# Softmax weights written to DRAM in pairs of steps and read back in 1 KB pieces

## The chip, the cores and the metric

The kernel runs on one core of one Trainium2 chip. The metric is the device time of one execution in microseconds (us). The core has five engines that run side by side: TensorE (PE in the profile, with its weight loads listed as PEld), VectorE (DVE), ScalarE (ACT), GpSimd (POOL) and SyncE (SP), which here issues nearly all DMAs. All arrays are float32.

## The reference

The kernel computes x + s * g for x of shape 2048 x 512. s is attention over a cached window, g the silu of a gated MLP with a mixing matrix over the positions. Cut to what matters here:

```
xn = layernorm(x)                                  # (2048, 512)
# s: 32 heads of size 128, keys and values: the last 512 of the cache
q = xn @ wq                                        # per head (2048, 128)
p = softmax(q @ k.T * 128 ** -0.5)                 # per head (2048, 512)
s = concat(p @ v) @ wo                             # (2048, 512)
# g
z = gelu(xn @ w_in);  z1, z2 = halves of z         # 688 columns each
g = silu((z1 * (w_sp @ layernorm(z2) + b_sp)) @ w_out)
return x + s * g
```

The change concerns p alone, on its way from the softmax to p @ v.

## The kernel before

**Numbers.** Each matmul of float32 accuracy is three: every operand is split into a high part (float32r, made by a cast on ScalarE) and a rest (what is left, made by a subtraction, `rest`, L59). `mm3` (L63 to L67) issues high x high, high x rest and rest x high into one PSUM buffer.

**Stages.** After layernorm and the first products of z the attention runs from about 55 to 1500 us of the span. The mixing and the output follow (after 1500 us); they aren't touched by the change.

**Blocks and steps.** The attention works on 128 blocks, each one head and 512 queries, and each block has four steps of 128 queries. There are 512 steps; one loop (L672 to L722) runs over them, and writes the order of the instructions by hand: nothing is reordered by a scheduler. A step's work is spread over several turns of that loop. For step t with t = 4b + j:

- `score(t)` (turn t, L466 to L475): three matmuls give 128 queries x 512 keys in PSUM. VectorE takes the row maximum (nm), ScalarE the exponential into the tile prob and the row sums. The division by the sums is left to the end.
- `turn(t)` (turn t + 1, L477 to L488): VectorE's transpose works on squares of 32 x 32, so it turns p within each square only, into the tile pB. SyncE writes pB to DRAM (p_dram, 4 x 128 x 512 for a block), 256 KB at a time, rows of 2 KB.
- `turned(b)` (turn 4b + 6, L490 to L494): four DMAs, one for each quarter of the keys, bring the block back so that the squares come to stand in their places: into 32 partitions each of the tile pL (keys on partitions, 2048 values each). A contiguous piece is 128 values, 512 bytes. In the loop `turned` stands ahead of `turn` of the same turn: the reads of block b are issued ahead of the write of step 1 of block b + 1.
- `shares(b, c)` (turn 4b + c + 10, L496 to L502): for each 128 keys ScalarE casts the high part (pT_h) out of pL, in runs of 32 values, and GpSimd makes the rest (pT_l).
- `pv(b, c)` (turn 4b + c + 12, L504): three matmuls for each quarter of the keys accumulate o, 128 columns of the head x 512 queries, in PSUM (ps_a). `pv_out` (L509) casts it to oT_h on ScalarE and appends the rest oT_l to a list `late`, which VectorE takes at the end of the turn, after its transpose.
- `outp(b, j)` (turn 4b + j + 17, L518): three matmuls with the head's wo; VectorE multiplies by the reciprocal sums and adds to sacc (L528).

Beside this, PE computes the next q (`q_products`, L437 to L447, a scheme of seven products over blocks of two heads), and GpSimd and ScalarE split the weights that are loaded for coming heads. The loads of weights (`load_piece`, L102, and `load_q`, L407), 256 KB each, stand at the head of a turn; the pieces of heads come at turns that are 0, 5 and 6 modulo 8, two pieces for q at 7 modulo 16. From turn 30 to 214 the second half of x is prepared and stored in DRAM (x_dram), and at turns 231 to 245 it is fetched.

**Queues.** All these DMAs go through SyncE's one queue, in the order of the program. SyncE waits for the buffers and data of a DMA before it issues it, and what comes after it in the program waits too.

**Buffers.** prob has 3 buffers, pB 4 of 2 KB per partition, p_dram 3 blocks, pL 2, pT_h and pT_l 4 each. The pool `ap` of these tiles has 2 buffers where a tile names no other number.

Of the kernel before, what the change touches and what calls it, by code (L numbers as in the profile page):

```python
# [8 lines left out]
F32 = mybir.dt.float32  # L9
# [8 lines left out]
P = 128  # L18
# [18 lines left out]
Q = 32  # L37
# [3 lines left out]
def mixer_kernel(ctx: ExitStack, tc: tile.TileContext, x, wh, w_in, w_sp, b_sp, w_out, out):  # L41
# [8 lines left out]
    nc = tc.nc  # L50
# [3 lines left out]
    dram = ctx.enter_context(tc.tile_pool(name="dram", bufs=1, space=DRAM))  # L54
# [3 lines left out]
    def rest(engine, lo, whole, hi):  # L58
        engine.tensor_tensor(lo, whole, hi.bitcast(F32), op=OP.subtract)  # L59

    late = []
# [25 lines left out]
    ap = att.enter_context(tc.tile_pool(name="ap", bufs=2))  # L87
# [259 lines left out]
    def z1_product(i, n, between=lambda: None):  # L347
        ps = ps_acc.tile([P, 512], F32, name="ps_a") if n else ps_step.tile([P, 512], F32, name="ps_3")
        zmm(ps[:, :NB], i, n, range(2))
        between()  # L350
        zmm(ps[:, :NB], i, n, range(2, NC))
        return ps
# [7 lines left out]
        z1_out(i, n, z1_product(i, n, between))  # L360


    qps, qT, pps, pD, pL, pT, oT, prob, sums = {}, {}, {}, {}, {}, {}, {}, {}, {}

    def where(b):
# [111 lines left out]
    def turn(t):  # L477

        b, j = divmod(t, 4)
        pB = ap.tile([P, 512], F32, name="pB", bufs=4)
        nc.vector.transpose(pB.rearrange("p (k q) -> p k q", q=Q), prob.pop(t))  # L483
        if j == 0:
            pD[b] = dram.tile([4, P, 512], F32, name="p_dram", bufs=3)
        nc.sync.dma_start(pD[b][j], pB)
        if j == 3:
            nc.vector.reciprocal(sums[b], sums[b])  # L488

    def turned(b):  # L490
        pL[b] = ap.tile([P, 16, P], F32, name="pL")
        of = pD.pop(b).rearrange("j (i r) (a f) -> a r (j i) f", i=4, a=4)
        for a in range(4):
            nc.sync.dma_start(pL[b][Q * a:Q * a + Q], of[a])  # L494

    def shares(b, c):  # L496
        hi = ap.tile([P, 512], F32R, name="pT_h", bufs=4)
        lo = ap.tile([P, 512], F32R, name="pT_l", bufs=4)
        p, h, l = pL[b][:, :, Q * c:Q * c + Q], *(t.rearrange("p (i q) -> p i q", q=Q) for t in (hi, lo))
        nc.scalar.copy(h, p)  # L500
        rest(nc.vector if 4 * b + c >= NSTEP - 10 and c % 2 else nc.gpsimd, l, p, h)
        pT[b, c] = (hi, lo)  # L502
# [6 lines left out]
    def pv_out(b, c):  # L509
        if c == 3:  # L510
            hi = ap.tile([P, 512], F32R, name="oT_h")
            lo = ap.tile([P, 512], F32R, name="oT_l")
            ps = pps.pop(b)
            nc.scalar.copy(hi, ps)
            late.append((rest, nc.vector, lo, ps, hi))
            oT[b] = (hi, lo)

    def outp(b, j):  # L518
# [74 lines left out]
    for p in range(4):  # L593
        seq, store = later_x(p)
        for f, ks in seq:
            t = 30 + 13 * n // 5
# [41 lines left out]
    ps = ps_step.tile([P, 512], F32, name="ps_3")  # L638
# [9 lines left out]
    ps = ps_step.tile([P, 512], F32, name="ps_3")  # L648
# [4 lines left out]
    ps = ps_acc.tile([P, 512], F32, name="ps_a")  # L653
# [18 lines left out]
    for t in range(T0, T1):  # L672
# [9 lines left out]
        i = t + XL  # L682
        if i < T8:
            ln_flip(i)
        if 0 <= bm < NBLK:
            shares(bm, cm)
# [10 lines left out]
        g, s = divmod(t + LEAD, 16)  # L697
# [6 lines left out]
        if t in DRAIN:  # L704
            ps = z1_product(*DRAIN[t])
# [4 lines left out]
        if 0 <= bp < NBLK:  # L710
            pv_out(bp, cp)
        if t in DRAIN:
            z1_out(*DRAIN[t], ps)
        if t % 4 == 2 and 0 <= t // 4 - 1 < NBLK:
            turned(t // 4 - 1)
        if 0 <= t - 1 < NSTEP:
            turn(t - 1)
# [7 lines left out]
    ps = z1_product(*LAST[-1])  # L725
# [276 lines left out]
```

## Time and profile before

| | us |
|---|---|
| median of 2 runs | 1877.19 (1876.64 to 1877.74) |
| the profiled execution | 1883.31 |
| its span, first to last instruction | 1881.4 |
| PE busy in the span | 1826.0 |
| VectorE busy | 1397.8 |
| GpSimd busy | 1243.4 |
| ScalarE busy | 1177.5 |

The profile is one execution; busy times are sums over an engine's instructions. Matmuls overlap, and their ends are modelled. The rows of the trace that the prediction quotes are of these kinds. A row of a stretch has its start and end, its length, the busy time and number of instructions of each engine (PE, PEld, VectorE, ScalarE, GpSimd, as far as they have any), the TensorE clock granted, the share of the 16 DMA engines and GB/s. A row of waits has who waited for whom, us in total, times, and the longest. A timeline row has start, length, engine, line, operation, out<-in and, after an x, how many in a row were merged. A GB/s row cuts a stretch into 40 equal slices. A row of a group of instructions has the shapes, the number, the busy time and mean ns of one, and the idle time of the engine ahead of it with what ended it. A row of DMA issues has the number, the size and the median us from issue to landing.

### The profile page before, as it was taken

The page shows a single profiled execution, that of the slowest core. Times are in us where ns is not written, and L with a number is a line of the kernel's source. Part 1 is how long each engine was busy: PE and PEld are TensorE (multiplying, and loading weights), DVE is VectorE, ACT ScalarE, POOL GpSimd, SP SyncE. Part 2 cuts the span into 40 slices and gives each one's busy share as a digit, 9 for nine tenths or more (in the row PEclk, how much of TensorE's full clock was granted, in tenths as well). Part 3 has the DMA queues.
Part 4 walks back from the last instruction along what each step waited for, and adds up shares of the span by engine and source line. Part 5 has one row for each costly group of instructions (what it writes and reads, how often), then busy time and mean ns, then how long its engine had stood idle before and what let it go on. Part 6 is the DMA issues. An engine that isn't in the chain of part 4 may idle for free.

```text
span 1881.4 us, 28888 instructions
## 1 busy us (share of the span) xinstructions
PE 1826.0 (97%) x8658; PEld 1549.1 (82%) x8658; DVE 1397.8 (74%) x2369; ACT 1177.5 (63%) x2631; POOL 1243.4 (66%) x1185
## 2 busy tenths in 40 slices
PE   8999999999999998899999999999999999999999
PEld 7777878878778776677888888888887899999998
DVE  5687988989889886788888888888887555333333
ACT  4666767767767765667777777777776444333322
POOL 3787888889888886778888888888886343000000
PEclk9999999999999999999999999999999999999999
DMA  5799999999999999999999999999999825554532
GB/s 178 194 288 239 241 273 246 267 260 265 256 257 241 255 253 293 247 271 247 262 240 253 254 248 248 242 256 249 260 236 260 238 92 164 164 168 139 179 114 89
DMA packets 445565, 429.22 MB, mean 228 GB/s; under 512 B 26368, under 2 KB 318976, under 8 KB 444256
## 3 DMA queue, kind: packets, MB, share of 16 engines
q1 hardware_dynamic: 440800, 421.74, 84.3%
q10 hardware_dynamic: 4608, 5.64, 0.9%
q8 instruction: 68, 1.11, 0.2%
q14 instruction: 89, 0.73, 0.1%
HBM read 260.55 MB, written 166.72 MB: 227 GB/s over the span
## 4 chain that ended last, share of the span: by engine, by line
PE 71%; DMA 13%; ACT 5%; DVE 5%; POOL 3%; issue 3%; SPq 1%; ACTq 0%; POOLq 0%; DVEq 0%
PE ps_a L446 10%; PE ps L65 9%; PE ps L67 9%; PE ps L66 9%; PE ps_a L66 6%; DMA p_dram<-pB 6%; PE ps_a L67 6%; PE ps_a L65 6%; DMA pL<-p_dram 5%; PE ps_g L66 4%; PE ps_g L67 4%; PE ps_g L65 4%; ACT prob L475 2%; POOL pT_l L59 1%; DVE nm L473 1%
## 5 line engine op out<-in xcount | busy, mean ns | idle before, releaser
L59 POOL TENSOR_TENSOR pT_l<-pL,pT_h 128x512 fp32r<-128x512 f32 x507 | 658.3, 1299 | 248.4 <-ACT pT_h L500 160.7
L475 ACT ACTIVATE prob<-ps,nm 128x512 f32<-128x512 f32 x512 | 352.1, 688 | 218.7 <-DVE nm L473 215.3
L500 ACT CAST pT_h<-pL 128x512 fp32r<-128x512 f32 x512 | 317.5, 620 | 193.8 <-DMA pL<-p_dram 128.3
L528 DVE SCALAR_TENSOR_TENSOR sacc<-ps,sums,sacc 128x512 f32<-128x512 f32 x496 | 368.3, 743 | 93.1 <-PE ps L67 91.3
L483 DVE STREAM_TRANSPOSE pB<-prob 128x512 f32<-128x512 f32 x512 | 359.3, 702 | 77.5 <-DMA p_dram<-pB 65.5
L446 PE MATMUL ps_a<-x,x 128*128 128x512 f32 x1302 | 377.7, 390 | 0.6 <-DVE oT_l L59 0.4
L473 DVE TENSOR_REDUCE nm<-ps 128x1 f32<-128x512 f32 x512 | 340.2, 664 | 8.5 <-PE ps L67 8.5
L446 PEld LDWEIGHTS ps_a<-x,x 128*128 128x128 f32 x1302 | 245.2, 188 | 53.7 <-DVE oT_l L59 2.3
L59 POOL TENSOR_TENSOR wl<-raw,wh 128x512 fp32r<-128x512 f32 x192 | 249.9, 1302 | 9.0 <-ACT wh L141 9.0
L66 PE MATMUL ps_a<-pT_l,wh 128*128 128x512 f32 x512 | 205.7, 402 | 19.0 <-POOL pT_l L59 18.4
L65 PE MATMUL ps_a<-pT_h,wh 128*128 128x512 f32 x512 | 201.6, 394 | 19.3 <-ACT pT_h L500 19.3
L65 PE MATMUL ps<-wh,qT_h 128*128 128x512 f32 x512 | 202.1, 395 | 3.8 <-DVE sacc L528 2.5
L65 PE MATMUL ps<-wh,oT_h 128*128 128x512 f32 x512 | 200.4, 391 | 0.3 <-DVE sacc L528 0.3
L67 PE MATMUL ps<-wh,oT_l 128*128 128x512 f32 x512 | 200.4, 391 | 0.0
L67 PE MATMUL ps_a<-pT_h,wl 128*128 128x512 f32 x512 | 200.4, 391 | 0.0
L66 PE MATMUL ps<-wl,qT_h 128*128 128x512 f32 x512 | 200.2, 391 | 0.0
L67 PE MATMUL ps<-wh,qT_l 128*128 128x512 f32 x512 | 200.2, 391 | 0.0
L66 PE MATMUL ps<-wl,oT_h 128*128 128x512 f32 x512 | 200.2, 391 | 0.0
L66 PE MATMUL ps_g<-z_l,x 128*128 128x344 f32 x512 | 164.5, 321 | 1.1 <-POOL z_l L59 1.1
L67 PE MATMUL ps_g<-z_h,x 128*128 128x344 f32 x512 | 164.5, 321 | 0.0
L65 PE MATMUL ps_g<-z_h,x 128*128 128x344 f32 x512 | 164.3, 321 | 0.0
L66 PEld LDWEIGHTS ps_a<-pT_l,wh 128*128 128x128 f32 x512 | 96.4, 188 | 56.7 <-POOL pT_l L59 38.2
(203 smaller groups left out, 3229.1 us busy)
## 6 DMA issues: line engine op xcount, KB each, us to landing
p_dram<-pB SPq DMA_DIRECT2D x512, 256.0 KB, 6.0
pL<-p_dram SPq DMA_DIRECT2D x512, 256.0 KB, 5.4
raw<-wh SPq DMA_DIRECT2D x194, 256.0 KB, 6.2
wq<-wh SPq DMA_DIRECT2D x62, 256.0 KB, 6.5
x<-w_sp SPq DMA_DIRECT2D x60, 256.0 KB, 5.8
x_dram<-rawx SPq DMA_DIRECT2D x32, 256.0 KB, 6.4
x<-x_dram SPq DMA_DIRECT2D x28, 256.0 KB, 6.6
u_dram<-uB SPq DMA_DIRECT2D x15, 384.0 KB, 2.3
```

The costliest lines, as they stand in the source:

```text
L59: engine.tensor_tensor(lo, whole, hi.bitcast(F32), op=OP.subtract)
L65: nc.tensor.matmul(ps, lh, rh, start=first, stop=False)
L66: nc.tensor.matmul(ps, lh, rl, start=False, stop=False)
L67: nc.tensor.matmul(ps, ll, rh, start=False, stop=last)
L446: nc.tensor.matmul(qps[g, bank], wt["q", g, k][a][:, c * P:(c + 1) * P], X[g * 2 // H][ORDER[k]][:, b, c], start=first, stop=r == 5, skip_ ...
L473: nc.vector.tensor_reduce(nm, ps, axis=AX.X, op=OP.max, negate=True)
L475: nc.scalar.activation(prob[t], ps, AF.Exp, bias=nm, accum_out=sums[b][:, j:j + 1])
L483: nc.vector.transpose(pB.rearrange("p (k q) -> p k q", q=Q), prob.pop(t))
L500: nc.scalar.copy(h, p)
L528: nc.vector.scalar_tensor_tensor(at, ps, rs, at, op0=OP.mult, op1=OP.add)
```

## The change

A pair of steps now shares one buffer. The tile pB holds, for each of the four quarters of the keys, 128 values of the even step and then 128 of the odd one; it has the pool's 2 buffers of 4 KB instead of 4 of 2 KB. It goes to DRAM after the odd step only, 512 KB at once, rows of 4 KB (p_dram is 2 x 128 x 1024). The four reads of a block take pieces of 256 contiguous values, 1 KB. The queries then stand in another order (two steps interleaved in groups of 32), the matmuls of pv carry that order along, and the casts of o write their results back into the right one. The rest of o is made in two halves.

```diff
+    pB = [None]
@@ turn
-        pB = ap.tile([P, 512], F32, name="pB", bufs=4)
-        nc.vector.transpose(pB.rearrange("p (k q) -> p k q", q=Q), prob.pop(t))
+        if j % 2 == 0:
+            pB[0] = ap.tile([P, 4, 2, P], F32, name="pB")
+        nc.vector.transpose(pB[0][:, :, j % 2, :].rearrange("p a (c q) -> p a c q", q=Q),
+                            prob.pop(t).rearrange("p (a c q) -> p a c q", a=4, q=Q))
         if j == 0:
-            pD[b] = dram.tile([4, P, 512], F32, name="p_dram", bufs=3)
-        nc.sync.dma_start(pD[b][j], pB)
+            pD[b] = dram.tile([2, P, 1024], F32, name="p_dram", bufs=3)
+        if j % 2:
+            nc.sync.dma_start(pD[b][j // 2], pB[0].rearrange("p a j f -> p (a j f)"))
@@ turned
-        pL[b] = ap.tile([P, 16, P], F32, name="pL")
-        of = pD.pop(b).rearrange("j (i r) (a f) -> a r (j i) f", i=4, a=4)
+        pL[b] = ap.tile([P, 8, 256], F32, name="pL")
+        of = pD.pop(b).rearrange("s (i r) (a f) -> a r (s i) f", i=4, a=4)
@@ shares
-        p, h, l = pL[b][:, :, Q * c:Q * c + Q], *(t.rearrange("p (i q) -> p i q", q=Q) for t in (hi, lo))
+        p = pL[b].rearrange("p i (j f) -> p (i j) f", j=2)[:, :, Q * c:Q * c + Q]
+        h, l = (t.rearrange("p (i q) -> p i q", q=Q) for t in (hi, lo))
@@ pv_out
-            ps = pps.pop(b)
-            nc.scalar.copy(hi, ps)
-            late.append((rest, nc.vector, lo, ps, hi))
+            ps = pps.pop(b).rearrange("p (s i j q) -> p s i j q", s=2, i=4, j=2)
+            h, l = (t.rearrange("p (s j i q) -> p s i j q", s=2, i=4, j=2) for t in (hi, lo))
+            nc.scalar.copy(h, ps)
+            for k in range(2):
+                late.append((rest, nc.vector, l[:, k], ps[:, k], h[:, k]))
```

## The prediction

> **What bounds the kernel now.** The page first: the attention stage (slices 2 to 31, about 55 to 1475 us) has PE at 8 to 9 tenths and DMA at 9. Then busy time by stretch, where x counts instructions.
>
> ```profile
> span 1881.4 us, 28888 instructions
> 100.00:900.00 800.00, 764.48 (x3283) 613.54 (x3282) 666.67 (x1132) 555.34 (x1303) 657.17 (x627) 0.99 1.00 259
> 900.00:1400.00 500.00, 500.00 (x2206) 413.81 (x2205) 440.86 (x735) 368.49 (x853) 436.30 (x404) 1.00 0.97 249
> 1400.00:1500.00 100.00, 94.66 (x456) 79.32 (x455) 69.71 (x112) 58.73 (x132) 57.65 (x49) 1.00 0.94 250
> ```
>
> The first numbers are PE, then weight loads, VectorE, ScalarE, GpSimd. From 900 to 1400 us PE is never idle: 2206 matmuls at 0.227 us each. At that rate the 3283 of 100 to 900 us need 744 us and took 800: 56 us are lost there. The same query for the tile pB counts steps:
>
> ```profile
> 100.00:900.00 800.00, 196.30 (x280) 0.99 1.00 259
> 900.00:1400.00 500.00, 132.88 (x190) 1.00 0.97 249
> ```
>
> So 70 blocks of four steps take 11.4 us each in the first part, and 47.5 blocks take 10.53 us in the second. What PE waits for (100 to 1450 us):
>
> ```profile
> PE ps_a L65 <- ACT pT_h L500: 18.6, 10, 5.9
> PE ps_a L66 <- POOL pT_l L59: 15.5, 35, 0.9
> ```
>
> Both are casts of p that came back late, so the round trip of p through DRAM limits the first part. SyncE's own timeline shows that trip; all its transfers go through one queue.
>
> ```profile
> 1000.41 2.23 SPq L486 DMA_DIRECT2D p_dram<-pB  x2
> 1005.77 1.91 SPq L494 DMA_DIRECT2D pL<-p_dram  x4
> 1007.73 2.36 SPq L486 DMA_DIRECT2D p_dram<-pB  x3
> 1010.13 0.46 SPq L102 DMA_DIRECT2D raw<-wh  x1
> 1012.33 0.32 SPq L486 DMA_DIRECT2D p_dram<-pB  x1
> 1012.74 0.38 SPq L102 DMA_DIRECT2D raw<-wh  x1
> 1015.01 1.91 SPq L494 DMA_DIRECT2D pL<-p_dram  x4
> 1016.97 0.49 SPq L486 DMA_DIRECT2D p_dram<-pB  x1
> 1017.50 1.56 SPq L407 DMA_DIRECT2D wq<-wh  x2
> 1019.16 0.40 SPq L486 DMA_DIRECT2D p_dram<-pB  x1
> 1019.60 0.43 SPq L102 DMA_DIRECT2D raw<-wh  x1
> 1020.78 2.96 SPq L486 DMA_DIRECT2D p_dram<-pB  x2
> 1026.94 1.03 SPq L494 DMA_DIRECT2D pL<-p_dram  x2
> ```
>
> A closed loop: the four reads of a block (1005.77) wait until its step 3 has landed; behind them come steps 1, 2, 3 of the next block (x3 from 1007.73), and that step 3 releases the next reads (1015.01). Step 0 is written while SyncE would else only wait (1012.33): its transfer lies in the gap between the release and the first read bytes. Two turns took 9.24 + 11.93 = 21.17 us, with three weight loads ahead of the releases (two wq, one raw).
>
> ```profile
> raw<-wh SPq DMA_DIRECT2D x194, 256.0 KB, 6.2
> wq<-wh SPq DMA_DIRECT2D x62, 256.0 KB, 6.5
> x_dram<-rawx SPq DMA_DIRECT2D x32, 256.0 KB, 6.4
> x<-x_dram SPq DMA_DIRECT2D x28, 256.0 KB, 6.6
> ```
>
> 256 loads are four per two blocks; the program's order puts two of them behind the release. So an average pair has one load fewer ahead of it than this one. What the queue moves per 0.2 us from 1005 us on:
>
> ```profile
> GB/s 123 21 31 20 0 0 0 0 23 61 133 146 287 348 330 307 215 189 182 169 179 187 197 205 264 223 195 207 205 202 189 177 174 210 202 236 307 399 379 430
> ```
>
> Zeros are the turnaround; then the reads burst to 348 and settle at about 200 GB/s; the writes at the end run at about 400. So 256 KB of 2 KB packets are 0.262 MB / 0.4 = **0.655 us**, and the reads of a block 1.049 MB / 0.2 = **5.24 us**. The loop, first by its turns: (21.17 - 0.655) / 2 = 10.26 us. Then by parts: reads 5.24, three writes 1.97, one load 0.66, turnaround 2.1 (step 3's bytes end about 0.655 before step 0's, at some 1004.5; the reads' first are at 1006.6), sum 9.97. So it is 0.27 to 0.56 us shorter than PE's 10.53: I take 0.4 us of **slack**. In the first part the 60 extra transfers of x alone add 60 x 0.655 / 70 = 0.56 us a block, and the slack is gone.
>
> **The change, part by part.**
>
> *Step 0 waits for step 1.* The pair 0/1 is issued where step 1 was, behind the reads. Step 0's 256 KB leave the gap and stand in the loop: **+0.655 us** a block. The pair 2/3 moves the same bytes as before, and step 3 still releases. SyncE's order is otherwise unchanged; the weight loads keep their places, and those behind the release still fill the gap.
>
> *1 KB pieces.* If the pieces' size set the reads' rate, it would have been slow from the first packet on. It isn't: 348 GB/s for some 0.6 us, then 200. It also rises to 264 GB/s for one slice (at 1009.8), a little past the half, where the reads turn from partitions 32 to 63 to partitions 64 to 127. That looks like a limit at the written end, with some 0.1 MB buffered ahead of it. The nearest row with larger pieces are the reads of u, 768 bytes, also 32 partitions each, from 1680 us on in 0.1 us:
>
> ```profile
> GB/s 399 430 185 0 0 0 0 0 0 0 0 0 0 0 0 0 0 54 131 154 238 238 185 131 123 261 300 223 161 154 238 215 223 131 253 318 387 397 405 451
> uL<-u_dram SPq DMA_DIRECT2D x4, 96.0 KB, 2.2
> ```
>
> The middle of it again averages some 200 GB/s (its four small issues may hold it back too). So a read gains between nothing and what the first 0.2 us slices allow; I bound it by 220 GB/s, the plateau's upper slices: 4.77 us, 0.47 less; the far end, a price per packet, is the first rival. A loss is excluded: the same bytes go to the same places in half the packets. I take 0.13, near the equal rates.
>
> The Trainium skill (SBUF — State Buffer, "Door 1: The DMA port swizzle") says that partitions 0 to 31 reach only 8 of the 16 ports, measured at 189 GB/s for 1 MiB, with about 218 as the asymptote; the plateau above agrees, and by this rule the piece size is worth at most the 0.47. Against it stands DMA: Bandwidth & Descriptors, "Why small descriptors are slow (HBM only)", with some 3 cycles per packet beside 32 bytes a cycle: 512 bytes take 19 cycles and 1 KB 35, an estimate of 8% or 0.4 us off the reads, which would leave +0.25 a block.
>
> *Two pair buffers for four single ones* (the default two of the pool). The transpose of a block's step 0 now waits until the pair 0/1 before it has landed. VectorE's timeline, the landing of the write issued at 1007.73, and this wait's sum over the run so far (us, times, longest):
>
> ```profile
> 1001.60 0.70 DVE L483 STREAM_TRANSPOSE pB<-prob 128x512 f32<-128x512 f32 x1
> 1009.03 0.70 DVE L483 STREAM_TRANSPOSE pB<-prob 128x512 f32<-128x512 f32 x1
> 1011.60 0.70 DVE L483 STREAM_TRANSPOSE pB<-prob 128x512 f32<-128x512 f32 x1
> 1014.25 0.70 DVE L483 STREAM_TRANSPOSE pB<-prob 128x512 f32<-128x512 f32 x1
> DMA to landing us min/median/max: 5.9/5.9/5.9
> DVE pB L483 <- DMA p_dram<-pB: 65.5, 37, 8.1
> ```
>
> It lands at 1013.6; its buffer (step 1's) is wanted at 1014.25, 0.6 later. With pairs it is wanted at 1011.60, with 0.655 more to move: 2.7 us late. VectorE has (500 - 440.9) / 47.5 = 1.24 us idle a block. Behind the waiting transpose stand the rests, the next score's maximum (ScalarE's exponential waits for it) and the update of sacc (PE waits for that buffer). Below nothing a gain is excluded: a buffer is given up. I take nothing, since in the first part blocks are 0.9 us longer and step 0 comes later; the other end is the second rival.
>
> *The casts of o.* The rest of o becomes two halves. Rows from 480 to 700 us, and the page's cast of p, which reads runs of 32:
>
> ```profile
> L59 DVE TENSOR_TENSOR oT_l<-ps_a,oT_h 128x512 fp32r<-128x512 f32 x20 | 13.7, 684 | 8.3 <-ACT oT_h L514 8.1
> L59 DVE TENSOR_TENSOR rawx<-ps,rawx 128x256 fp32r<-128x256 f32 x4 | 1.4, 395 | 0.0
> L500 ACT CAST pT_h<-pL 128x512 fp32r<-128x512 f32 x512 | 317.5, 620 | 193.8 <-DMA pL<-p_dram 128.3
> ```
>
> 2 x 395 - 684 = 0.106 us, 128 times: 14 us of VectorE, hidden in its idle time; without that cover up to 14. The cast of o writing runs of 32 should cost between nothing and 0.1 us of ScalarE (which idles 245 us of the first 800), and the transposes into strided runs, by four blocks of 128 elements, the same 0.70. The 256 SyncE issues saved are worth nothing: SyncE waits anyway.
>
> **Sum.** Per block +0.655 - 0.13 = +0.52 us. First part 70 x 0.52 = 36. From 900 to 1475 us 55 blocks x (0.52 - 0.4) = 7. Together +43. The profiled execution took 1883.3 (span 1881.4 and 1.9 around it), so 1926; the median of the runs is 6.1 lower: **1920 us**, 2.3% slower.
>
> **The rivals.**
>
> *The piece size counts: faster.* The queue's packets, 900 to 1400 us and 1600 to 1850 us:
>
> ```profile
> q1 hardware_dynamic: 141591, 124.11, 97.1%
> ```
> ```profile
> q1 hardware_dynamic: 23387, 36.93, 45.8%
> ```
>
> Packets, MB, share of 16 engines. 7768 and 1832 engine-us solve to 25.6 ns a packet and 33.4 ns a KB. A block's reads go from 2048 packets to 1024: -1024 x 0.0256 / 16 = -1.64 us, with step 0's write -0.98 a block. Of the 56 us lost in the first part and some 5 after 1400 us perhaps 42 come back: 1835. For it: DMA at 9 tenths with small packets. Against it: burst and plateau. Chance 0.15.
>
> *VectorE waits for the pair buffer: slower still.* At L483, from the point where the write lands later than step 0's transpose plus idle time. A block longer by s cuts the wait to 2.7 - s and raises idle time to 1.24 - 0.11 + s, so s = 0.78 us in the second part: 55 x 0.78 = 43; the first part's blocks are long enough already and keep the 36. 1877 + 79 = 1956. Against it: the release may come earlier once VectorE is late. Chance 0.22.
>
> *The pieces stay as they were* (split again on the way): 70 x 0.655 + 55 x 0.255 = 60, 1937. Both ends of each piece are 256 contiguous elements, so only 0.05.
>
> **How the numbers follow.** The forecast has 0.58; its own range runs from 1890 (relief 0.47: 70 x 0.185 = 13, and the slack covers the second part) to 1937 (no relief). A measurement of this kernel can tell about 2% from no change: below 1839.6 or above 1914.7. Slower: 0.22 + 0.05 + 0.26 of the forecast's 0.58 (its upper half) = 0.53. Faster: half of the first rival, 0.08. Within: 0.39. The range leaves out about 0.1 on each side: 1850, between the first rival and the forecast, to 1965, just over the second rival.
>
> **What would show it.** Right: 256 writes of 512 KB; queue 1 down by 131072 + 32768 packets; the read plateau still near 200 GB/s; the distance from read to read longer by half a us; more of PE's wait on pT_h; 900 to 1400 us no longer free of PE idle time. The second rival: VectorE's wait of pB on p_dram far above 65.5 us, and PE waiting on sacc or prob. Wrong: if the plateau rises towards 300 GB/s, or PE's idle time before 900 us shrinks.

## The result, and the profile after

The changed kernel takes 1964.99 us (median of 2 runs, 1964.18 to 1965.79) against 1877.19: 4.7% slower, ratio 1.0468, 95% interval 1.0423 to 1.0513. The prediction said 1920, so the direction holds, and of the 88 us it had 43. The measured time lies at the upper end of the stated range (1850 to 1965), which was set there for the second rival.

First the page's span line, then busy time by stretch of the changed kernel (PE, weight loads, VectorE, ScalarE, GpSimd), then the same stretches for the tile pB alone, where the x counts steps.

```profile
span 1964.0 us, 28248 instructions
100.00:900.00 800.00, 737.70 (x3142) 588.05 (x3141) 636.46 (x1151) 539.02 (x1249) 632.65 (x600) 0.99 0.91 248
900.00:1400.00 500.00, 476.29 (x2032) 381.24 (x2031) 406.24 (x723) 342.75 (x788) 403.37 (x372) 0.99 0.86 230
```
```profile
100.00:900.00 800.00, 187.26 (x267) 0.99 0.91 248
900.00:1400.00 500.00, 122.94 (x176) 0.99 0.86 230
```

From 900 to 1400 us PE did 2206 matmuls before and does 2032 now. A block of four steps took 800 / 70 = 11.43 us in the first stretch and 500 / 47.5 = 10.53 in the second; now it is 800 / 66.75 = 11.99 and 500 / 44 = 11.36. So the loss is 0.56 us a block early and 0.83 late: 70 x 0.56 + 55 x 0.83 = 85 us, nearly all of the 88. One step more or fewer in a stretch moves these numbers by about 0.05 us. The DMA share fell from 1.00 and 0.97 to 0.91 and 0.86: the queue has more idle time, and the kernel is slower.

Who waits for whom in the changed kernel from 100 to 1450 us (us in all, times, longest):

```profile
DVE pB L485 <- DMA p_dram<-pB: 206.1, 96, 7.3
PE ps L65 <- DVE sacc L535: 79.6, 80, 6.0
```

Before, VectorE waited 65.5 us there, and PE waited for late casts of p. Now PE waits for VectorE's updates of sacc, which stand behind the waiting transpose in VectorE's order. The page's chain of work that ended last, by engine, shows the same shift (before, then after); in it the writes of p alone (p_dram<-pB) went from 6% to 32%:

```profile
PE 71%; DMA 13%; ACT 5%; DVE 5%; POOL 3%; issue 3%; SPq 1%; ACTq 0%; POOLq 0%; DVEq 0%
DMA 37%; PE 34%; DVE 16%; ACT 6%; issue 4%; SPq 2%; POOL 1%; ACTq 0%; DVEq 0%; POOLq 0%
```

One such wait in the timelines of SyncE and of VectorE (start, length, what; in brackets the idle time ahead and its releaser):

```profile
1002.22 0.32 SPq L490 DMA_DIRECT2D p_dram<-pB  x1
1006.33 1.80 SPq L498 DMA_DIRECT2D pL<-p_dram  x4
1008.23 4.32 SPq L490 DMA_DIRECT2D p_dram<-pB  x2
1012.59 1.26 SPq L102 DMA_DIRECT2D raw<-wh  x2
1017.69 0.33 SPq L498 DMA_DIRECT2D pL<-p_dram  x1
```
```profile
1006.89 0.69 DVE L485 STREAM_TRANSPOSE pB<-prob 128x512 f32<-128x512 f32 x1
1008.74 0.70 DVE L485 STREAM_TRANSPOSE pB<-prob 128x512 f32<-128x512 f32 x1
1011.48 0.70 DVE L485 STREAM_TRANSPOSE pB<-prob 128x512 f32<-128x512 f32 x1
1016.11 0.71 DVE L485 STREAM_TRANSPOSE pB<-prob 128x512 f32<-128x512 f32 x1 [1.87 <-DMA p_dram<-pB]
```

Step 1's transpose (1006.89) completes the pair 0/1 at 1007.6, while SyncE issues the four reads. The pair goes out at 1008.23, behind them, and lands 7.8 us later; the pair 2/3 before it (1002.22) had landed 4.0 us after its issue. The next step 0 is the transpose at 1016.11; it stood for 1.87 us until the write of 1008.23 had landed. Over the whole span VectorE waits 106 times for a landing, and 103 of these are step 0's. From read to read it is now 1017.69 - 1006.33 = 11.36 us.

The packets changed as described, and the reads did not get faster. The page's issue rows and queue row (packets, MB, share), and what the queue moves per 0.2 us from 1006 us on:

```profile
p_dram<-pB SPq DMA_DIRECT2D x256, 512.0 KB, 6.8
pL<-p_dram SPq DMA_DIRECT2D x512, 256.0 KB, 5.6
q1 hardware_dynamic: 272864, 421.72, 76.9%
```
```profile
GB/s 0 0 0 0 0 0 26 36 148 179 343 369 333 230 154 159 195 169 118 128 205 195 236 184 159 230 266 266 210 230 241 200 220 277 328 435 394 389 410 410
```

There are 167,936 packets fewer. The reads burst to 369 GB/s and then run, from 1008.6 to 1012.6, at 200 GB/s on average: the same plateau with pieces of 1 KB as with 512 bytes. That is one block. From 900 to 1400 us the reads of p alone move packets of 512 bytes (1 KB with the change), so their rate can be taken over all blocks there: without the first 7% and the last 3%, a block's packets move at 202 GB/s before and 198 after (mean of 48 and 44 blocks).

### The profile page after: what moved, and what is told of

Read it like the earlier page. It is cut to its first block, busy times and chain, and to the rows that moved or that the text cites. A ratio compares the mean times of both kernels' runs of the same rounds, so it can differ in the third digit from the quotient of the medians.

```text
span 1964.0 us, 28248 instructions
## 1 busy us (share of the span) xinstructions
PE 1851.8 (94%) x8658; PEld 1551.2 (79%) x8658; DVE 1394.3 (71%) x2497; ACT 1187.8 (60%) x2631; POOL 1250.5 (64%) x1185
## 4 chain that ended last, share of the span: by engine, by line
DMA 37%; PE 34%; DVE 16%; ACT 6%; issue 4%; SPq 2%; POOL 1%; ACTq 0%; DVEq 0%; POOLq 0%
DMA p_dram<-pB 32%; DVE nm L474 5%; PE ps_g L67 4%; PE ps_g L66 4%; PE ps_g L65 4%; DVE pB L485 4%; DVE sacc L535 3%; DMA pL<-p_dram 3%; PE ps L65 3%; PE ps_a L65 3%; PE ps_a L66 3%; PE ps_a L447 3%; PE ps_a L67 2%; PE ps L67 2%; PE ps L66 2%
## 5 line engine op out<-in xcount | busy, mean ns | idle before, releaser
L65 PE MATMUL ps<-wh,qT_h 128*128 128x512 f32 x512 | 213.6, 417 | 86.8 <-DVE sacc L535 81.2
L65 PEld LDWEIGHTS ps<-wh,qT_h 128*128 128x128 f32 x512 | 97.2, 190 | 147.8 <-DVE sacc L535 94.7
```

Of the source, the lines that this page charges most:

```text
L65: nc.tensor.matmul(ps, lh, rh, start=first, stop=False)
```

## The experiments

Two theories went in. The **loop** theory is the forecast's: step 0's 256 KB now stand between a block's reads and the next release. The **buffer** theory is the second rival: with two pair buffers VectorE waits for a write that stands behind the reads.

**e1: three single buffers in the kernel before.** This gives step 0 the deadline that it has with the pairs, with nothing else of the change. The other steps get their buffers back one step later too, but in the trace 97 of VectorE's 102 waits for a landing are step 0's.

```diff
-        pB = ap.tile([P, 512], F32, name="pB", bufs=4)
+        pB = ap.tile([P, 512], F32, name="pB", bufs=3)
```

> The kernel before with three single buffers for pB instead of four: step 1's buffer is now wanted by step 0 of the next block, the deadline that the pairs have, with nothing else of the change. Buffer theory (VectorE waits for a buffer whose write stands behind the reads): in the kernel before that write lands 14.15 us after the end of step 3's transpose (mean of blocks 72 to 117) and step 0's next transpose starts at 12.25, so it is 1.9 us late; two blocks take at least 14.15 + 7.9 (start of step 0 to end of step 3 at VectorE's pace, from the changed kernel), 11.0 us a block against 10.53: 1905 to 1940 us, VectorE's wait of pB on p_dram over 150 us. Loop theory (step 0's write, moved ahead of the next release, is the whole cost): step 0's write is where it was, so 1877, within 8 us.

Measured: 1987.55 us, ratio 1.0602 (1.0570 to 1.0633). The waits, 100 to 1450 us:

```profile
DVE pB L483 <- DMA p_dram<-pB: 192.7, 92, 6.4
PE ps L65 <- DVE sacc L528: 91.0, 69, 6.1
```

One 2 KB buffer fewer costs more than the whole change and leaves the same two waits. This agrees with the mechanism of the buffer theory, but its size was too low (it gave 1940 at most). The loop theory's 1877 doesn't fit.

**e2: the pairs alone**, with 512-byte pieces (the added lines, the transpose cut).

```diff
+        if j % 2 == 0:
+            pB[0] = ap.tile([P, 2, 512], F32, name="pB")
+        nc.vector.transpose(pB[0][:, j % 2, :]...., prob.pop(t))
+        if j % 2:
+            nc.sync.dma_start(pD[b][j - 1:j + 1].rearrange("j p f -> p j f"), pB[0])
```

> The kernel before with the pairs alone: two steps share a buffer (2 buffers) and go to DRAM in one write of 512 KB, rows of 2 KB; DRAM layout, the 512-byte reads and the casts of o are as before. If the piece size is worth nothing (reads limited where they are written): as the changed kernel, 1955 to 1980. If a packet has a price of 25.6 ns, a block's reads are 1.64 us longer than with 1 KB pieces, half of which shows in a loop over two blocks: 1964 + 125 x 0.8 = 2060, and at 8% shorter reads (0.4 us) some 1990.

Measured: 1979.31 us, ratio 1.0558 (1.0533 to 1.0583). Its steps in the two stretches:

```profile
100.00:900.00 800.00, 185.52 (x264) 0.97 0.97 245
900.00:1400.00 500.00, 122.98 (x175) 1.00 0.94 230
```

The pairs alone are as slow as the change, or some 0.9% slower (1.0558 against 1.0468). Pieces of 1 KB, rows of 4 KB and the other casts together give back 800 / 66 - 800 / 66.75 = 0.14 us a block early and 500 / 43.75 - 500 / 44 = 0.06 late, which is three steps and one. A price per packet would have given 0.8.

**e3: three pair buffers**, with the space taken from two other tiles.

```diff
-            pB[0] = ap.tile([P, 4, 2, P], F32, name="pB")
+            pB[0] = ap.tile([P, 4, 2, P], F32, name="pB", bufs=3)
-        prob[t] = ap.tile([P, W], F32, name="prob", bufs=3)
+        prob[t] = ap.tile([P, W], F32, name="prob", bufs=2)
-            t = qps[g, "t", k] = ap.tile([P, 512], F32, name="qs", bufs=3)
+            t = qps[g, "t", k] = ap.tile([P, 512], F32, name="qs", bufs=2)
```

> The changed kernel with three pair buffers; the 4 KB per partition for it come from prob (2 buffers instead of 3) and qs (2 instead of 3). Buffer theory: the pair is wanted two steps later, at 17.2 + 2 us instead of 15, well after it lands (14.9), VectorE's wait on p_dram falls under 30 us. What is left then is the loop theory's share: with it 1900 to 1925 us, without it 1870 to 1885. If the time stays over 1950, neither the buffer nor VectorE's wait was the cause.

Measured: 1937.35 us, ratio 1.0337 (1.0318 to 1.0356), over the 1925 that the loop theory allowed. VectorE's wait is gone, and another one has taken its place (waits, 100 to 1450 us; then the steps; then SyncE's timeline):

```profile
DVE pB L485 <- DMA p_dram<-pB: 2.3, 1, 2.3
ACT pT_h L505 <- DMA pL<-p_dram: 223.1, 94, 7.4
PE ps_a L66 <- POOL pT_l L59: 29.6, 60, 0.9
PE ps_a L65 <- ACT pT_h L505: 16.1, 11, 3.2
```
```profile
100.00:900.00 800.00, 191.26 (x272) 0.98 0.90 252
900.00:1400.00 500.00, 126.52 (x180) 1.00 0.85 236
```
```profile
1003.66 1.81 SPq L498 DMA_DIRECT2D pL<-p_dram  x4
1005.51 0.45 SPq L490 DMA_DIRECT2D p_dram<-pB  x1
1006.00 1.55 SPq L408 DMA_DIRECT2D wq<-wh  x2
1007.60 0.87 SPq L102 DMA_DIRECT2D raw<-wh  x1
1008.56 0.45 SPq L490 DMA_DIRECT2D p_dram<-pB  x1
1015.69 1.80 SPq L498 DMA_DIRECT2D pL<-p_dram  x4
```

PE waits for casts of p again. After the reads of 1003.66 everything up to the next release is issued by 1009; SyncE then has nothing to do until 1015.69, when the last of it has landed. That is the loop as the forecast drew it, 500 / 45 = 11.11 us a block late, 0.58 over the kernel before.

**e4: the changed kernel with the pair ahead of the reads.**

```diff
-        if t % 4 == 2 and 0 <= t // 4 - 1 < NBLK:
-            turned(t // 4 - 1)
         if 0 <= t - 1 < NSTEP:
             turn(t - 1)
+        if t % 4 == 2 and 0 <= t // 4 - 1 < NBLK:
+            turned(t // 4 - 1)
```

> The changed kernel with the pair 0/1 of the next block issued ahead of the reads of a block, not behind them (turn before turned in the loop). The reads then wait for step 1's transpose, at about 5.3 us after step 3's, when they are released anyway (5.65). The pair lands at 5.3 + 0.8 + 1.3 + 0.8 = 8 to 9 us instead of 14.9, before the next step 0 wants its buffer (12.3). Buffer theory and loop theory both: the wait and the longer loop go, 1845 to 1885 us. If the place of that write is not the cause: 1965 or more, since the reads come later by the 1.3 us of that write.

Measured: 1880.44 us, ratio 1.0032 (1.0011 to 1.0053). Two lines moved take back nearly all of the loss, with the pieces, the pairs and the two buffers left as they are. Both theories asked for this; it shows that the place of that write behind the reads is what both of them hang on.

**e5: the control for e3**, the kernel before with prob and qs at two buffers.

> Control for e3: the kernel before with prob at 2 buffers and qs at 2 instead of 3 each, nothing of the change. If these two cost nothing, 1873 to 1885, and the 64 us by which e3 is over the kernel before belong to the change. If they cost 30 us or more, most of what e3 still loses is theirs, and the loop theory's share is small.

Measured: 1878.55 us, ratio 0.9999 (0.9983 to 1.0015). The borrowed buffers cost nothing.

**e6: the kernel before with step 1's write ahead of the reads** (the edit of e4).

> The kernel before with step 1's write issued ahead of the reads of the block before (turn before turned), nothing else. Loop theory: 256 KB leave the way from reads to release, the loop is 0.655 us shorter; 900 to 1400 us is limited by PE already and stays at 10.5 us a block, the first part gains up to 0.655 x 70 = 46 us of the 56 that it loses: 1830 to 1860. If the loop doesn't set the first part (only the bursts of x do), 1868 to 1880.

Measured: 1875.17 us, ratio 0.9982 (0.9964 to 1.0001). A miss for the loop theory, which gave 1860 at most. But the edit does not only shorten the way from read to release: the reads now also wait until step 1 has been transposed. From 100 to 1450 us SyncE waits 321.9 us for a landing ahead of the reads and 140.2 us for a transpose ahead of a write in the kernel before; in e6 it is 86.7 and 355.6 us. Most of the wait for the landing came back as a wait for VectorE. So the place of that write is worth nothing in the kernel before; that a shorter loop is worth nothing there isn't shown.

**e7: the reads in another order**, in the kernel before.

```diff
-        for a in range(4):
+        for a in (0, 2, 1, 3):
             nc.sync.dma_start(pL[b][Q * a:Q * a + Q], of[a])
```

> The kernel before with the four reads of a block issued in the order of quarters 0, 2, 1, 3 instead of 0, 1, 2, 3: partitions 0-31, 64-95, 32-63, 96-127. Same pieces, same bytes. If the written end limits the reads by halves (partitions 0-63 and 64-127 each have their own limit, with about 0.1 MB buffered ahead), each change of half gives a short burst: three instead of one, the reads of a block 0.2 to 0.5 us shorter, 1850 to 1870. If the limit is per packet or in DRAM, the order does nothing: 1873, within 5.

Measured: 1855.19 us, ratio 0.9863 (0.9831 to 0.9895). What the queue moves per 0.2 us from 1000 us on, the reads issued at 999.9, and the steps in the two stretches:

```profile
GB/s 10 0 0 41 64 131 212 251 328 264 254 271 233 236 215 192 172 169 177 212 212 190 197 169 184 215 238 215 218 238 200 279 374 399 420 389 420 369 440 379
```
```profile
100.00:900.00 800.00, 203.01 (x289) 0.99 0.99 267
900.00:1400.00 500.00, 132.60 (x189) 1.00 0.94 251
```

The same 512-byte packets now run at 215 to 328 GB/s for 1.6 us before they fall to the plateau; the three short bursts of the expectation aren't seen. This one block's reads are no shorter than those of the block shown before. Over all blocks from 900 to 1400 us they are: the same 90% of the packets move at 216 GB/s instead of 202, some 0.3 us less for a block. Packet size and bytes are unchanged, so neither sets the plateau. The order of the written partitions does, or the order of the quarters in DRAM, which changes with it; that it is the written end fits, but e7 doesn't separate the two. All the gain in time is early, 289 steps for 280; late PE is the limit either way.

**e8: the rest of o in two halves**, in the kernel before.

```diff
-            late.append((rest, nc.vector, lo, ps, hi))
+            for k in range(2):
+                late.append((rest, nc.vector, *(u[:, 256 * k:256 * k + 256] for u in (lo, ps, hi))))
```

> The kernel before with the rest of o made in two halves of 256 columns, nothing else. 0.11 to 0.14 us more of VectorE a block, hidden in its 1.24 us idle time: 1873 to 1878. If VectorE were the bound already, 0.14 x 128 = 18 us more.

Measured: 1877.80 us, ratio 0.9990 (0.9974 to 1.0006). Hidden, as worked out.

**e9: e3 with the edit of e4**, three pair buffers and the pair first.

> e3 (the changed kernel with three pair buffers) with the pair 0/1 issued ahead of the reads. It takes away what e3 still has of the change's longer way, the 512 KB between the reads and the next release, and leaves the pieces of 1 KB, the writes of 512 KB and the casts. Loop theory: 1865 to 1880, blocks of 10.5 us from 900 to 1400 us instead of e3's 11.15. If e3's loss is due to the larger writes as such (they land later) or to the casts, it stays over 1920.

Measured: 1885.17 us, ratio 1.0051 (1.0032 to 1.0071), 5 us over the loop theory's 1880. The steps:

```profile
100.00:900.00 800.00, 198.78 (x284) 0.99 0.97 262
900.00:1400.00 500.00, 130.57 (x186) 1.00 0.94 245
```

500 / 46.5 = 10.75 us a block late where e3 had 11.11. So most of e3's loss was the place of the write, not its size, its later landing or the casts. A third buffer is worth nothing once the write is early (e4: 1.0032). The half per cent that stays in both was not taken apart.

**e10 to e12: towards a faster kernel.** e10 is e9 with the order of e7; e11 is the kernel before with e6 and e7 together; e12 is the kernel before with the reads in eight parts:

```diff
-        for a in range(4):
-            nc.sync.dma_start(pL[b][Q * a:Q * a + Q], of[a])
+        for k in range(2):
+            for a in (0, 2, 1, 3):
+                nc.sync.dma_start(pL[b][Q * a:Q * a + Q, 8 * k:8 * k + 8], of[a][:, 8 * k:8 * k + 8])
```

> e9 with the reads in the order of quarters 0, 2, 1, 3. If the halves of the partitions limit the reads, about as much comes off as in e7 (23 us): 1845 to 1858. The best form of the change that I know; if 1 KB pieces are worth anything with that limit eased, it falls below e7's 1855.

> The kernel before with both: step 1's write ahead of the reads, and the reads in the order 0, 2, 1, 3. e6 was worth nothing and e7 23 us; if they don't depend on each other, 1850 to 1858. If the shorter read leaves the place of the write as the next limit, 1840 to 1850.

> The kernel before with each block's reads in eight transfers of 128 KB, queries in two halves, each half in the order of quarters 0, 2, 1, 3: seven changes of half instead of e7's three, pieces still 512 bytes. If the halves limit the reads and some 0.1 MB is buffered, the two limits now work side by side nearly all the time: a block's reads 0.5 us or more shorter than in e7, 1840 to 1855. If SyncE's issue time (8 x 0.48 = 3.8 us) or small transfers cost it, 1855 to 1890.

Measured: e10 1861.64 us, ratio 0.9922 (0.9901 to 0.9943); e11 1852.73, ratio 0.9879 (0.9857 to 0.9902); e12 1839.70, ratio 0.9808 (0.9787 to 0.9830). The change in its best form (e10) gains from the order too, but misses its 1858 and stays behind the kernel before with the same two edits (e11): even with the read limit eased the 1 KB pieces bring nothing to be seen in the time. The reads themselves run at 220 GB/s in e10 and 218 in e11 (the same 90%, 900 to 1400 us). e11 isn't told apart from e7. e12, with pieces of 512 bytes in transfers half as large, beats all; its stretches and its queue from 1007 us on, the eight reads issued from 1007.59:

```profile
100.00:900.00 800.00, 787.95 (x3439) 646.30 (x3438) 696.38 (x1184) 582.20 (x1363) 688.81 (x655) 0.99 0.96 270
900.00:1400.00 500.00, 499.51 (x2203) 412.95 (x2202) 441.53 (x738) 369.72 (x858) 436.97 (x402) 1.00 0.92 253
```
```profile
GB/s 164 266 277 276 256 328 358 399 269 248 254 126 159 333 282 294 272 151 202 208 282 264 243 230 187 123 184 292 284 284 254 266 228 353 392 405 379 359 154 154
```

3439 matmuls in the first 800 us against 3283. The reads share these slices with some writes. The row has repeated stretches at 250 to 330 GB/s, but the read packets alone, over all blocks from 900 to 1400 us, move at 219 GB/s, no faster than in e7 (216). So what e12 gains beyond e7 isn't the rate of the reads. It has smaller transfers, and its writes of p land 3.6 us after their issue (median, 900 to 1400 us) where e7 has 5.6; the cause was not taken apart.

## Why the prediction was right or wrong

Two steps of the prediction failed, and they share the missing 45 us about equally: the slack (the loop alone cost some 63 us where 43 were forecast) and the two pair buffers (some 25 us where nothing was taken). The signs that the prediction named agree: the distance from read to read grew, but more of PE's wait on pT_h did not come, and the signs of the second rival did.

*Step 0 leaves the gap and stands in the loop: +0.655 us a block.* Right as a mechanism, and nearly right in size. e3 has it without the buffer wait: +0.33 us a block early (800 / 68 against 11.43) and +0.58 late; e9 takes the write out of the way, and most of it goes.

*The slack of 0.4 us.* This is the first step that failed. It let only 0.12 of 0.52 through from 900 to 1400 us; e3 shows 0.58 there. Two turns of the loop and a list of parts gave 0.27 and 0.56, and the middle of two rough figures was taken. PE was always busy in that stretch, but that told nothing of how near the second limit was. e3's 11.11 us less 0.655 is 10.45: the loop stood within 0.1 us of PE's 10.53 if all of e3's loss there is the loop's, and within 0.3 if the 0.22 that e9 keeps is not.

In the first stretch it went the other way: there 0.52 was counted in full, and 0.33 came. By blocks that is 23 us against the forecast's 36 early, and 32 against 7 late, so the two errors partly cancel. Why less came early is argued, not shown. The DMA engines are busy for 1.00 of that stretch, and e7 and e12, which change only the reads, gain only there; that speaks for the work in the queue as the limit, and not for the length of the loop. e6, which should have settled it, put another wait in the place of the one it removed. As the loop's cost alone the forecast's +43 stands against e3's 3.4%, some 63 us.

*Two pair buffers: "I take nothing".* This is the second step that failed. The working beside it had the write 2.7 us late against 1.24 us of idle time, and then set it aside because blocks are longer in the first part and step 0 comes later. The trace of the kernel before shows that this reason doesn't hold. From 900 to 1400 us the next block's write of step 1 lands 14.1 us after the end of a block's step 3 transpose (mean), and the step 0 that would want its buffer with the pairs starts 12.2 us after that end: 1.9 us too early. From 100 to 900 us it is 16.0 and 13.2 us, so 2.9. Where blocks are longer the write lands later still. With the change VectorE waits 206 us instead of 65.5, PE's waits have moved to VectorE, and from e3 to the changed kernel 1.0337 becomes 1.0468: some 25 us beyond the loop. e1 shows that the deadline without the longer loop is enough to cost 6%. The second rival, with 1956 us and a chance of 0.22, came nearest; it gave the late part 0.78 us a block (measured 0.83, loop included) but nothing of its own to the early part. That the early part shows 0.56 for the 0.52 forecast is luck: 0.33 of it is the loop's, the rest the buffers'.

The two limits do not add: e1, which has the deadline without the longer loop, is slower than the changed kernel, which has both. Why was not tried; in both it is step 0 that waits.

*1 KB pieces: 0.13 us, near nothing.* Right. e2 bounds all that the pieces, the rows and the casts bring at 0.06 to 0.14 us a block. The read packets say the same (the 90% as above, 900 to 1400 us): 198 GB/s with 1 KB against 198 in e2, 202 to 204 (e9, e4) against 200 in e6, 220 (e10) against 218 in e11. Taken from the 25% to the 95% mark, past the burst, e4 and e9 come out some 5% over e6, and the changed kernel still where e2 is; the 8% that the prediction set against its own view is not reached by either reading. The rival with a price per packet is refuted: at its 25.6 ns a packet and 33.4 ns a KB the 16 engines could move packets of 512 bytes at no more than some 192 GB/s and packets of 1 KB at some 274, and e7 has 216 with the former and the changed kernel 198 with the latter. The Trainium skill's rule on partitions and ports (SBUF — State Buffer, "Door 1: The DMA port swizzle") puts quarters 0 and 1 on one set of ports and 2 and 3 on the other, and the gain of e7 from that order alone agrees with it. The traces show the halves, not the ports.

*The casts and the transposes.* Right: 0.70 us a transpose as before, 0.58 us a cast of o as before (mean), and e8 finds nothing.

## What to carry to other kernels

Before two transfers are joined into one, look at what stands ahead of the joined one in its queue and when its buffer is wanted again: here joining moved the deadline one step forward, and a write behind 1 MB of reads could not meet it. Where two limits stand at nearly the same period, an engine that is always busy hides the second; a change that costs the second one even a little can then show almost in full, as it did here from 900 to 1400 us. A reason for setting a computed delay aside should be measured like the delay itself: the distance that decides is that from the landing to the next use, in each stretch. If a transfer runs at a steady plateau after a burst, try its order or its place before its piece size: here the order brought 1.4%, the size nothing.

## What the runs showed of the hardware

DMA reads from DRAM into 32 partitions settle at about 200 GB/s with pieces of 512 bytes and of 1 KB alike, while writes from 128 partitions behind them run at about 400. Four such reads in an order that changes between partitions 0 to 63 and 64 to 127 each time run at 216 GB/s instead of 202 (e7 against the kernel before, 900 to 1400 us), and the kernel takes 1.4% less. Eight transfers half as large in such an order are worth 1.9% (e12), though the reads are no faster (219).

In this kernel one buffer of 2 KB fewer for a tile that waits on a DMA costs 6% (e1); a buffer fewer for two tiles that engines alone pass on to each other (prob, qs) costs nothing (e5, 0.9999).
